# Conversions moved into attention, narrow gate products, and GpSimd's two-operand work given to VectorE

## The chip, the cores and the metric

The kernel runs on one core of a Trainium2 chip. The metric is the device time of one execution in microseconds (us). Engines are named as in the profile: PE is TensorE (matrix products, transposes), PEld its weight loads, DVE is VectorE, ACT is ScalarE, POOL is GpSimd, SP is SyncE, which here only issues transfers.

## The reference

Three layers follow each other.

```python
# 1. attention, 4 batches x 8 heads, 768 positions of 64 numbers:
#    a window of 15 neighbours on each side, and 24 block summaries (max of k, mean of v over 32 positions)
scores_all = concat([where(|i-j| < 16, q@k.T / 8, -1e9), q@k_sum.T / 8 + log(32)], -1)
x = softmax(scores_all) @ concat([v, v_sum])          # -> 3072 tokens x 512
# 2. mixture of 8 experts, each takes exactly 384 tokens, assigned greedily by descending gate value
logits = x @ w_gate                                    # 3072 x 8
out[mask_e] = relu(x[mask_e] @ w1[e]) @ w2[e]          # 512 -> 1024 -> 512
# 3. gated layer, all tokens
a, b = x @ moe2_w1, x @ moe2_w2                        # "gate weights" below: 512 x 1024 each, float64 inputs
y = ((a * b) @ moe2_w3) @ moe2_w_out                   # 1024 x 1024, 1024 x 512, float64 inputs
```

The matrices of layer 3 arrive in float64 and are turned into float32 on the core ("conversions"). The product of the two last ones, moe2_w3 @ moe2_w_out, is formed once on the core ("folds").

## The kernel before, in words

**The planner.** The kernel doesn't issue its instructions in the order of the program text. `body` describes every operation to `Plan`, with a due time (`at(t)`, in planned us) and a cost from `cost`. `Plan.run` then plays the engines forward on the host: whenever an engine is free it takes, among the operations whose inputs are ready, the one that is due first, and the order found is written out as fixed queues, one for each engine. Operations inside `urgent()` are "hot": an operation that isn't hot is held back if a hot one would become ready within `HOLD` ns while it ran. `SAFE`, `REL` and `LAG` are margins for semaphores and buffers: a buffer counts as free `REL` after its last reader, or `SAFE` for a VectorE operation that isn't hot and touches the routing's buffer `rt`.

**Attention.** 16 units (4 batches x 4 pairs of heads), each with three groups of four 64-row blocks. PE forms scores, transposes and outputs; ACT takes the exponential; POOL rearranges q and k. Behind each unit the gate product for its 128 columns is added into a PSUM tile `rt` (`GT`): six products of 128 tokens each, with the tokens' transposed values (`XT`, 128 x 128) as the stationary operand and the gate weights (128 x 8) as the moving one. Behind the fourth unit of a batch VectorE copies the tile to `LG`. Between these, spread over attention by due times, stand 32 conversions (`conv`) of 128 x 512 numbers: ACT and POOL take absolute values and limits, VectorE does two bit operations, POOL the last addition. Eight of them are for moe2_w_out, sixteen for moe2_w3 and 4 x `ND` = 8 for the gate weights, whose results are stored to device memory (`abd`).

**Behind attention.** `nc.swap` releases attention's buffers; operations described after it see `nc.bar` set. Then run, by due time: the routing of expert 0 (`routing(0)`, hot: six rounds of comparing on VectorE (`gq`), counting on PE, a new threshold (`need`, `ni`, `base`, `thr`, `pre`), then the list of tokens `idx`); seven folds (hot: transposes, 24 products of 512 columns, splits into a high and a low part on ACT and VectorE: `xh`, `xl`, `w`); the loads of the four stored gate weight rows (`load_ab`), each split by ACT (`ab`, high part) and POOL (low part); the remaining eight conversions (`conv_ab`), each followed by such a split. `AB0` and `ABD` set their due times. Expert 0's weights come by indirect transfers that POOL issues, as soon as the routing has named the expert.

**The experts.** Eight rounds of about 90 us: tokens gathered by `idx`, layer 1 and 2 of the expert (`l1`, `l2`), then the gate weights (`l3`) and the folded matrix (`l4`). Meanwhile the routing of the next expert runs, not hot. All recorded instructions have one line, L395, that of the planner's helper; they are told apart by their tiles.

Of the kernel before, what the change touches and what calls it, by code (L numbers as in the profile page):

```python
# [8 lines left out]
F32 = mybir.dt.float32  # L9
# [90 lines left out]
class Plan:  # L100
# [130 lines left out]
    def run(self):  # L231
# [22 lines left out]
        while todo:  # L254
            moved = False
            for e, (wait, q) in ready.items():
# [35 lines left out]
                    if e == "sync":  # L292
                        self.free[e] = max(t + dur, self.dma - DMA_AHEAD)
                slow = e == "vector" and i not in self.hots and any(b.name == "rt" for b in ops[i][3])
                heapq.heappush(ends, (done + (SAFE if slow else REL), i))
                order.append(i)
                self.done[i] = t
                todo -= 1
# [43 lines left out]
       "vector": {"tensor": 150, "scalar": 128, "gpsimd": 156, "sync": 120, "vector": 127},  # L342
       "gpsimd": {"tensor": 143, "scalar": 76, "vector": 80, "sync": 240}}

HOLD = 150.0

CALM, CALM_D = 500.0, 2000.0

# [2 lines left out]
SAFE = 600.0  # L351
# [95 lines left out]
def body(tc, q, k, v, w_gate, w1, w2, wa, wb, w3, wo, out):  # L447
# [22 lines left out]
    STEP, T0, TL, TE = 3.3, 243, 271, 87  # L470
    GATE, EARLY = 1, 0.0
    NF, TR, FT, FD = 1, 2, 245, 3
    NW, ND, AB0, ABD = 8, 2, 12, 3.9
    P_LD, P_MN, P_VL, P_PUT, P_VC, P_RL, P_TR, P_N = 24, 8, 14, 6, 11, 10, 10, 2
    P_ST, P_SC, P_C0, P_C1, P_CL, P_FO, P_FS = 8, 10, 10, 15, 6, 3, 5
    P_GA, P_SU, P_RW, P_W2, P_W20, P_RO, P_WC = 20, 16, 40, 16, 6, 15, 6
# [92 lines left out]
    with at(10):  # L569
        triu = cp.tile([128, 128], BF, name="triu")  # L570
        nc.vector.tensor_scalar(triu, jp, 0.0, None, op0=OP.is_gt)
        LG = cp.tile([128, C, E], F32, name="LG")
        WG = ap_.tile([128, DB, E], F32, name="wg")
        nc.sync.dma_start(WG, w_gate.rearrange("(c p) e -> p c e", p=128))


    def split_sb(hi, lo, raw, eng=None):
        nc.scalar.activation(hi, raw, AF.Copy)
        (eng or nc.gpsimd).tensor_tensor(lo, raw, hi.bitcast(F32), op=OP.subtract)

    def split_ps(hi, lo, ps):
        nc.scalar.activation(hi, ps, AF.Copy)
# [17 lines left out]
    def conv(src, r, h, dst, t, raw=None):  # L600

        with at(t - P_CL):
            if raw is None:
                stages.append(ap_.tile([128, 1024], F32, name="sta", bufs=2, fifo=True) if len(stages) % 2 else stage())
                raw = stages[-1]
            nc.sync.dma_start(raw.bitcast(I32), src[r * 128:(r + 1) * 128, h * 512:(h + 1) * 512].bitcast(I32))
        with at(t), nc.patient():
            w = raw.bitcast(I32).rearrange("p (a b) -> p a b", b=2)
            lo, hi = w[:, :, 0], w[:, :, 1]
            c = ap_.tile([128, 512], F32, name="ca", bufs=1) if nc.bar is None and len(stages) % 4 == 0 else ep.tile([128, 512], F32, name="a", bufs=3)  # L610
            nc.scalar.activation(c, hi.bitcast(F32), AF.Abs)
            nc.scalar.activation(lo, lo.bitcast(U32), AF.Copy, scale=2.0 ** -29)
            nc.gpsimd.tensor_scalar(c, c, 122879.9921875, 2.0 ** -15, op0=OP.min, op1=OP.max)
            a = c.bitcast(I32)
            nc.vector.tensor_scalar(a, a, 5, 2, op0=OP.logical_shift_left, op1=OP.logical_shift_right)
            nc.vector.scalar_tensor_tensor(a, hi, -1073741824, a, op0=OP.bitwise_and, op1=OP.bitwise_or)
            f = dst if dst is not None else c
            nc.gpsimd.tensor_tensor(f.bitcast(I32), a, lo, op=OP.add)
        return f

    WO, W3, WF = {}, {}, {}
# [119 lines left out]
    def group(G):  # L741
# [59 lines left out]
        if g == 2:  # L801
            with at(STEP * G + P_SC):
                if pr == 0:
                    GT[b] = pp.tile([128, 6, E], F32, name="rt", fifo=True)
                with nc.block():
                    for i in range(3):
                        for t in range(2):
                            nc.tensor.matmul(GT[b][:, 2 * i + t], XT[u, i][:, t], WG[:, pr], start=(pr == 0 and i + t == 0),
                                             stop=(pr == HP - 1 and i + t == 3))
        if pr == HP - 1 and g == 2:  # L810
            with at(STEP * G + P_SC):
                nc.vector.tensor_copy(LG[:, 6 * b:6 * b + 6, :], GT[b])

    for u in range(NU):
        prep(u)
# [505 lines left out]
```

## Time and profile before

| what | value |
|---|---|
| median of 3 runs | 1032.13 us (1030.18 to 1032.99) |
| the profiled execution, its own time | 1025.71 us |
| its span, first to last instruction | 1023.9 us |
| PE busy | 966.9 us (94%) |
| PEld busy | 877.7 us (86%) |
| DVE busy | 603.9 us (59%) |
| ACT busy | 409.8 us (40%) |
| POOL busy | 321.5 us (31%) |
| mean granted clock of TensorE | 0.982 of full speed |

Busy time is the union of an engine's instructions; PE's ends are modelled, so that two neighbouring products overlap in the list, and the time that one takes in a row of products is the distance of the starts. Attention runs from 0 to about 229 us, the stretch with the folds and the first routing from 229 to 298 us, the eight experts from there to the end.

### The profile page before, as it was taken

How to read it: one execution, taken by the hardware profiler on the slowest of the kernel's cores; microseconds unless marked ns; L12 is line 12 of the kernel's file. 1: busy time of each engine (PE TensorE's matmuls, PEld its weight loads, DVE VectorE, ACT ScalarE, POOL GpSimd, SP SyncE). 2: the span in 40 equal slices, each digit the busy share in tenths (PEclk: the TensorE clock that was granted, in tenths of full speed). 3: DMA queues.
4: the chain of work that ended last, by engine and by line, in shares of the span. 5: the costliest groups of instructions: out<-in, count | busy, mean ns of one | idle time of the engine just before them, and what ended most of it. 6: DMA issues, size and time to landing. Idle time of an engine off the chain costs nothing.

```text
span 1023.9 us, 17970 instructions
## 1 busy us (share of the span) xinstructions
PE 966.9 (94%) x6827; PEld 877.7 (86%) x6827; DVE 603.9 (59%) x1620; ACT 409.8 (40%) x961; POOL 321.5 (31%) x401
## 2 busy tenths in 40 slices
PE   6798989997989999999999999999999999999995
PEld 5688978775678899989989998998999899999994
DVE  5775576858877853882685388268538726323210
ACT  5786878864343233233223323222332323223211
POOL 9986466646623221041022104102210414001001
PEclk9998999998999999999999999999999999999998
DMA  8767778772141311040131105003110405101000
GB/s 235 193 181 204 207 210 257 208 232 112 32 164 42 125 52 52 1 165 31 33 121 54 52 2 165 32 32 111 65 52 1 165 21 165 42 11 52 1 1 31
DMA packets 81703, 100.06 MB, mean 98 GB/s; under 512 B 30416, under 2 KB 63696, under 8 KB 81616
## 3 DMA queue, kind: packets, MB, share of 16 engines
q1 hardware_dynamic: 68560, 52.76, 18.3%
q0 software_dynamic: 13056, 46.14, 13.6%
q8 instruction: 54, 0.88, 0.3%
q14 instruction: 33, 0.27, 0.1%
HBM read 81.81 MB, written 14.68 MB: 94 GB/s over the span
## 4 chain that ended last, share of the span: by engine, by line
PE 57%; issue 10%; DVE 7%; DMA 4%; ACT 2%; POOL 2%; POOLq 0%; ACTq 0%; SPq 0%; DVEq 0%
PE mm L395 32%; PE ac L395 23%; DMA ra<-in_moe_w_dram,iw 3%; PE rt L395 2%; POOL ra L1109 1%; DVE wl L395 1%; DVE gq L395 1%; DVE a L395 1%; DVE xl L395 1%; DMA abd<-ca 1%; ACT s L395 1%; DMA st<-in_moe_w_dram,iw 1%; DVE base L395 1%; ACT wh L395 1%; DVE pre L395 0%
## 5 line engine op out<-in xcount | busy, mean ns | idle before, releaser
L395 PE MATMUL mm<-xh,ab 128*128 128x384 f32 x1024 | 273.4, 338 | 0.0
L395 PEld LDWEIGHTS mm<-xh,ab 128*128 128x128 f32 x1024 | 185.5, 188 | 4.5 <-issue 3.3
L395 PE MATMUL mm<-xl,ab 128*128 128x384 f32 x512 | 174.4, 341 | 0.0
L395 PE MATMUL ac<-w,hh 128*128 128x512 f32 x384 | 123.6, 398 | 0.0
L395 DVE TENSOR_TENSOR a<-a,mm 128x384 f32<-128x384 f32 x64 | 35.2, 551 | 140.4 <-PE mm L395 117.9
L1109 POOL DMA_INDIRECT ra<-in_moe_w_dram,iw x32 | 31.4, 982 | 219.3 <-DVE go L395 190.9
L395 PEld LDWEIGHTS mm<-xl,ab 128*128 128x128 f32 x512 | 96.1, 188 | 3.0 <-DVE xl L395 1.1
L395 PE MATMUL mm<-xh,wh 128*128 128x384 f32 x256 | 88.1, 345 | 0.8 <-ACT xh L395 0.7
L395 PE MATMUL mm<-xl,wh 128*128 128x384 f32 x256 | 87.0, 340 | 0.0
L395 PE MATMUL ac<-hl,wh 128*128 128x384 f32 x256 | 87.0, 340 | 0.0
L395 PE MATMUL ac<-hh,wl 128*128 128x384 f32 x256 | 86.8, 339 | 0.0
L395 PE MATMUL mm<-xh,wl 128*128 128x384 f32 x256 | 86.6, 338 | 0.0
L395 ACT ACTIVATE a<-mm 128x384 f32<-128x384 f32 x64 | 31.3, 490 | 137.6 <-PE mm L395 137.6
L1109 POOL DMA_INDIRECT xg<-xd,idx x24 | 35.3, 1472 | 158.6 <-PE mm L395 119.4
L395 PE MATMUL ac<-hh,wh 128*128 128x384 f32 x256 | 84.5, 337 | 0.0
L1171 POOL DMA_INDIRECT out_dram<-a,idx x24 | 26.7, 1114 | 176.9 <-ACT a L395 173.7
L395 PEld LDWEIGHTS ac<-w,hh 128*128 128x128 f32 x384 | 70.9, 188 | 11.8
L395 ACT ACTIVATE hh<-a 128x384 fp32r<-128x384 f32 x64 | 33.5, 524 | 115.7 <-DVE a L395 115.7
L395 DVE TENSOR_TENSOR wl<-st,wh 128x512 fp32r<-128x512 f32 x64 | 44.0, 688 | 57.7 <-ACT wh L395 57.5
L395 PE MATMUL ac<-w,hl 128*128 128x512 f32 x192 | 76.4, 398 | 0.0
L395 DVE TENSOR_TENSOR wl<-ra,wh 128x512 fp32r<-128x512 f32 x64 | 43.9, 687 | 41.7 <-ACT wh L395 41.7
L395 ACT ACTIVATE wh<-ra 128x512 fp32r<-128x512 f32 x64 | 42.4, 664 | 62.2 <-PE mm L395 32.7
(271 smaller groups left out, 2078.8 us busy)
## 6 DMA issues: line engine op xcount, KB each, us to landing
st<-in_moe_w_dram SPq DMA_DIRECT2D x14, 512.0 KB
sta<-in_moe_w_dram SPq DMA_DIRECT2D x14, 512.0 KB
kn<-in_k_dram SPq DMA_DIRECT2D x32, 192.0 KB
qn<-in_q_dram SPq DMA_DIRECT2D x32, 192.0 KB
xd<-xo SPq DMA_DIRECT2D x16, 384.0 KB
vw<-in_v_dram SPq DMA_DIRECT2D x32, 176.0 KB
vw<-vs SPq DMA_DIRECT2D x64, 36.6 KB
st<-in_moe_w_out_dram SPq DMA_DIRECT2D x4, 512.0 KB
```

The costliest lines, as they stand in the source:

```text
L395: return getattr(real_engine, method)(*map(real, a), **{k: real(x) for k, x in kw.items()})
L1109: nc.add("gpsimd", lambda: tc.nc.gpsimd.indirect_dma_start(out=real(dst), out_offset=None, in_=real(src), in_offset=bass.IndirectOffsetOnA ...
L1171: s = tc.nc.gpsimd.indirect_dma_start(out=out, out_offset=bass.IndirectOffsetOnAxis(ap=real(idx), axis=0), in_=real(o), in_offset=None)
```

## The change

Four things change.

1. `ND` goes from 2 to 3: twelve of the sixteen gate weights' conversions stand in attention (36 conversions there in all), six instead of four rows are loaded by `load_ab`, and four instead of eight conversions are left behind. Their due times move back by 10 us (`AB0`). The staging tiles of those left all come from the pool `ep`.
2. The gate products are turned round: the gate weights, padded to 32 columns, are the stationary operand, and 256 tokens' values the moving one; three products for each unit write 32 partitions each of `GT`. Behind the fourth unit the result is copied to SBUF by ACT, transposed back by two transposes on PE and copied to `LG` by VectorE.
3. Behind attention (`nc.bar` set) the low parts of the splits and the last addition of a conversion run on VectorE instead of POOL.
4. The planner holds non-hot operations for a hot one that comes within 300 instead of 150 ns, and counts the routing buffer `rt` as free three times `SAFE` (1800 ns) behind a VectorE operation that isn't hot.

```diff
-                heapq.heappush(ends, (done + (SAFE if slow else REL), i))
+                heapq.heappush(ends, (done + (3 * SAFE if slow else REL), i))
...
-HOLD = 150.0
+HOLD = 300.0
...
-    NW, ND, AB0, ABD = 8, 2, 12, 3.9
+    NW, ND, AB0, ABD = 8, 3, 22, 3.9
...
-        WG = ap_.tile([128, DB, E], F32, name="wg")
-        nc.sync.dma_start(WG, w_gate.rearrange("(c p) e -> p c e", p=128))
+        WG = ap_.tile([128, DB, 32], F32, name="wg")
+        nc.gpsimd.memset(WG, 0.0)
+        nc.sync.dma_start(WG[:, :, 0:E], w_gate.rearrange("(c p) e -> p c e", p=128))
...
     def split_sb(hi, lo, raw, eng=None):
         nc.scalar.activation(hi, raw, AF.Copy)
-        (eng or nc.gpsimd).tensor_tensor(lo, raw, hi.bitcast(F32), op=OP.subtract)
+        (eng or (nc.gpsimd if nc.bar is None else nc.vector)).tensor_tensor(lo, raw, hi.bitcast(F32), op=OP.subtract)
...
-                stages.append(ap_.tile([128, 1024], F32, name="sta", bufs=2, fifo=True) if len(stages) % 2 else stage())
+                stages.append(ap_.tile([128, 1024], F32, name="sta", bufs=2, fifo=True) if nc.bar is None and len(stages) % 2 else stage())
...
             f = dst if dst is not None else c
-            nc.gpsimd.tensor_tensor(f.bitcast(I32), a, lo, op=OP.add)
+            (nc.gpsimd if nc.bar is None else nc.vector).tensor_tensor(f.bitcast(I32), a, lo, op=OP.add)
...
-                    GT[b] = pp.tile([128, 6, E], F32, name="rt", fifo=True)
+                    GT[b] = pp.tile([128, 256], F32, name="rt", fifo=True)
                 with nc.block():
                     for i in range(3):
-                        for t in range(2):
-                            nc.tensor.matmul(GT[b][:, 2 * i + t], XT[u, i][:, t], WG[:, pr], start=(pr == 0 and i + t == 0),
-                                             stop=(pr == HP - 1 and i + t == 3))
+                        nc.tensor.matmul(GT[b][32 * i:32 * i + 32], WG[:, pr], XT[u, i].rearrange("p t s -> p (t s)"),
+                                         start=(pr == 0), stop=(pr == HP - 1))
         if pr == HP - 1 and g == 2:
             with at(STEP * G + P_SC):
-                nc.vector.tensor_copy(LG[:, 6 * b:6 * b + 6, :], GT[b])
+                lt = ap_.tile([96, 256], F32, name="lt", bufs=1)
+                nc.scalar.activation(lt, GT[b][0:96], AF.Copy)
+                ps = pp.tile([128, 2, 96], F32, name="mm", bufs=3)
+                for t in range(2):
+                    nc.tensor.transpose(ps[:, t, :], lt[:, t * 128:(t + 1) * 128], ident[0:96, 0:96])
+                nc.vector.tensor_copy(LG[:, 6 * b:6 * b + 6, :].rearrange("p (g t) e -> p g t e", t=2),
+                                      ps.rearrange("p t (g r) -> p g t r", r=32)[:, :, :, 0:E])
```

## Rows read from the trace of the kernel before

**Rows 1.** Windows: stretch, its length; PE, PEld, DVE, ACT, POOL busy; PEclk, DMA share, GB/s.

```profile
50.00:215.00 165.00, 153.53 (x1829) 136.14 (x1829) 111.94 (x224) 132.04 (x402) 108.19 (x149) 0.95 0.77 211
...
229.00:298.00 69.00, 57.56 (x321) 41.38 (x322) 61.85 (x143) 30.92 (x55) 38.62 (x32) 0.95 0.31 111
...
298.00:331.00 33.00, 30.62 (x188) 29.34 (x188) 22.08 (x65) 11.43 (x21) 7.73 (x7) 0.95 0.17 53
...
388.00:478.00 90.00, 89.49 (x547) 82.88 (x546) 55.81 (x176) 26.23 (x50) 16.19 (x17) 1.00 0.19 65
```

**Rows 2.** Timeline of VectorE, 229 to 298 us: start, duration, operation, [idle before].

```profile
229.14 0.21 DVE L395 COPY LG<-rt 128x48 f32<-128x48 f32 x1 [3.95 <-PE rt L395]
...
243.15 3.36 DVE L395 TENSOR_TENSOR gq<-key,thr 128x768 bf16<-128x768 f32 x2
...
287.58 0.15 DVE L395 SCALAR_TENSOR_TENSOR idx<-i 128x3 int32<-128x3 f32 x1
```

**Rows 3.** Timeline of TensorE, 229 to 298 us, same columns.

```profile
245.29 0.33 PE L395 MATMUL rt<-oh,gq 128*128 128x16 bf16 x6 [5.04 <-DVE gq L395]
...
297.77 1.41 PE L395 MATMUL mm<-xh,wh 128*128 128x384 f32 x3 [0.69 <-ACT xh L395]
```

**Rows 4.** Groups of VectorE, 229 to 298 us.

```profile
L395 DVE TENSOR_TENSOR gq<-key,thr 128x768 bf16<-128x768 f32 x9 | 10.0, 1120 | 0.0
...
L395 DVE TENSOR_TENSOR pre<-js,base 128x32 int32<-128x32 int32 x4 | 3.9, 977 | 0.1
...
L395 DVE SCALAR_TENSOR_TENSOR a<-ab,a 128x512 int32<-128x512 int32 x4 | 3.7, 930 | 0.1
L395 DVE SCALAR_TENSOR_TENSOR base<-ni,base 128x1 int32<-128x1 int32 x4 | 3.7, 915 | 0.1
L395 DVE TENSOR_TENSOR wl<-ra,wh 128x512 fp32r<-128x512 f32 x5 | 3.3, 681 | 0.0
L395 DVE TENSOR_SCALAR a<-a 128x512 int32<-128x512 int32 x4 | 2.4, 604 | 0.0
```

**Rows 5.** Groups of VectorE, 478 to 568 us, where GpSimd has no two-operand work.

```profile
L395 DVE TENSOR_TENSOR gq<-key,thr 128x768 bf16<-128x768 f32 x8 | 7.5, 952 | 0.0
...
L395 DVE TENSOR_TENSOR pre<-js,base 128x32 int32<-128x32 int32 x4 | 0.8, 190 | 0.1
...
L395 DVE SCALAR_TENSOR_TENSOR base<-ni,base 128x1 int32<-128x1 int32 x4 | 0.6, 160 | 0.1
```

**Rows 6.** Groups of GpSimd, 230 to 298 us.

```profile
L395 POOL TENSOR_TENSOR ab<-ab,ab 128x512 fp32r<-128x512 f32 x8 | 11.2, 1410 | 7.0 <-ACT ab L395 7.0
L395 POOL TENSOR_TENSOR ab<-a,ab 128x512 fp32r<-128x512 f32 x6 | 8.3, 1405 | 3.3 <-ACT ab L395 3.3
```

**Rows 7.** Timeline of TensorE inside attention, 154 to 162 us.

```profile
154.97 0.49 PE L395 MATMUL mm<-ident,kr 128*128 128x128 f32 x3
155.39 0.88 PE L395 MATMUL mm<-vw,ind 96*32 96x130 f32 x24
156.19 0.69 PE L395 MATMUL ac<-vw,pt 121*64 121x65 f32 x16
...
159.32 1.50 PE L395 MATMUL rt<-wg,xt 128*128 128x8 f32 x12
160.68 0.42 PE L395 MATMUL mm<-ident,xo 128*128 128x128 f32 x2
160.93 0.49 PE L395 MATMUL mm<-ident,qr 128*128 128x128 f32 x3
161.26 0.37 PE L395 MATMUL ac<-mv,sel 67*128 67x480 bf16 x1
```

**Rows 8.** Groups of GpSimd, 0 to 229 us: count, busy us, mean ns, idle before.

```profile
L395 POOL TENSOR_SCALAR a<-a 128x512 f32<-128x512 f32 x26 | 16.5, 635 | 9.8 <-ACT a L395 8.0 <-DVE rs L395 0.9
...
L395 POOL TENSOR_TENSOR a<-a,st 128x512 int32<-128x512 int32 x8 | 10.8, 1346 | 2.4 <-ACT pt L395 1.8 <-ACT sta L395 0.7
```

**Rows 9.** Who waited for whom on TensorE, 345 us to the end: total, times, longest.

```profile
PE rt L395 <- DVE i L395: 3.0, 5, 0.8
```

## The prediction

> **What bounds the kernel now.** I first cut the span into stages with the windows view [rows 1]. From 388 to 478 us, one expert of seven alike, TensorE is busy for 89.5 of 90 us at its full clock: nothing but its own work can be gained there. In attention (50 to 215 us) it is busy for 153.5 of 165 us, with ScalarE at 132, VectorE at 112 and GpSimd at 108: several engines are near their limit and TensorE is nearest. From 229 to 298 us it idles for 11.4 of 69 us, and its granted clock averages 0.95, so about 6.9 us ran at 1.2 instead of 2.4 GHz. VectorE is busy for 61.9 of those 69 us, 90%. That stretch is where the kernel loses time.
>
> Then the timelines. The stretch begins with the last copy of gate values at 229.14; the routing delivers the token list at 287.58, 58.4 us later [rows 2], and expert 0's first product starts at 297.77 [rows 3]. TensorE's queue is fixed and holds routing products between fold products, so when the routing is late the folds stand behind it: at 245.29 it had waited 5.04 us for the comparisons `gq`, two of which took 3.36 us together [rows 2, 3].
>
> The same instructions by group show why. In the stretch `pre` takes 977 ns, `base` (one number per partition) 915 and `gq` 1120 [rows 4]; in an expert's round, where GpSimd does nothing with two operands, they take 190, 160 and 952 [rows 5]. In the stretch GpSimd runs 14 low parts of splits of 1.4 us each [rows 6]. An instruction of VectorE with two operands in SBUF seems to stand until GpSimd's has ended.
>
> **The change part by part.**
>
> *Gate products.* A block of six now takes 160.68 - 159.32 = 1.36 us [rows 7]. The nearest row for the new form is the block for the means: also 32 columns wide and f32, twelve products of 130 columns over four column groups, in 156.19 - 155.39 = 0.80 us [rows 7]. That is three rounds of 0.267 us, four products side by side. One round of 256 columns is 0.267 x 256/130 = 0.53 us, and the three new products write three different groups, so I take 0.53; if they ran one behind the other it would be 1.58. Sixteen blocks save 13.4 us of TensorE, or cost 3.5. Eight new transposes at 0.11 us (three in 0.33, 161.26 - 160.93 [rows 7]) cost 0.9. TensorE frees 12.5 us.
>
> How much of that shortens attention? All, if TensorE alone set the pace; but it idles for 11.5 of 165 us already, waiting for others, and ScalarE stands at 80% [rows 1]. I take a third, 4 us. On the path to the routing the last product is 0.83 us shorter, while a copy by ScalarE and two transposes (0.22) come ahead of the 0.21 us copy [rows 2]; I put this at nothing, give or take 0.8.
>
> The three transposes in front of the narrow block take 155.39 - 154.97 = 0.42 us, the three in front of a full-width product 0.33 [rows 7]: entering the narrow form costs some 0.09 us. The Trainium skill, page TensorEngine Tiling (Array Packing), section Key Properties, says that a change of tiling mode drains TensorE. By that rule each new block pays twice; at 0.09 us that is 32 x 0.09 = 2.9 us of the 12.5, a third of it in the sum, which would then be 1 us later. I leave it out, since a fixed queue may set the block next to another narrow one.
>
> *Four more conversions in attention.* Each costs GpSimd 0.635 + 1.346 = 1.98 us [rows 8], the most of any engine, together 7.9. GpSimd is busy for 66% of 50 to 215 us and the transfers for 77% [rows 1], so most of it hides there; if that cover were gone, all 7.9 us would show. I take a fifth, 1.5 us. Each also brings a load and a store on SP's queue, ahead of which nothing waits but later loads. Attention in sum: 4 - 1.5 = 2.5 us earlier; bounds 12.5 earlier and 7.9 later (11.4 if the narrow products don't overlap).
>
> *GpSimd's two-operand work on VectorE.* It gives back the time in which VectorE stood: four `pre` at 0.79, four `base` at 0.755, nine `gq` at 0.17: 7.7 us [rows 4, 5], nearly all of it in the chain of the routing. Behind it goes TensorE's wait of 5.04 us [rows 3] and the low clock after it. What TensorE could gain at most from 229 to 331 us is its idle time, 11.4 + 2.4, and half of the time at the lower clock, 3.4 + 1.7: 18.9 us [rows 1].
>
> VectorE pays for it. A low part with 512 columns takes it 0.68 us, as `wl` does [rows 4]; sixteen are 10.9 us, four last additions 2.7. Two of the conversions that are left disappear, (0.604 + 0.930) x 2 = 3.1 us [rows 4]. From 229 to 331 us it has 61.9 + 22.1 = 84.0 us of work [rows 1]; afterwards 84.0 - 7.7 + 10.9 + 2.7 - 3.1 = 86.8. At the 90% that it reached in the stretch, this fits into 96.8 instead of 102 us: only 5.2 us come out. But the new work is due 10 us later and is not hot, so it can fill the 10.9 us that VectorE idles from 298 to 331 us [rows 1], and expert 1's routing, needed only for the round after, can slip. Between 5.2 and 18.9 I take 9, nearer the bound by VectorE. What is late next is the first product of `l3`, which needs all sixteen splits. Fewer loads or more of them change little: the transfers are busy for 31% there [rows 1].
>
> *The planner.* The longer margin for `rt` moves routing products in the experts' rounds back in TensorE's queue. Five waits of TensorE for `i` are 3.0 us [rows 9], and they are the only ones recorded there. I take 2 of the 3, bounds 0 and 3. The longer hold acts on hot neighbours only, in the stretch, and is inside the 9.
>
> *Sum.* 2.5 + 9 + 2 = 13.5 us. The profiled execution took 1025.71 us, its span plus 1.8 for what lies around it; that is 6.4 us below the median of 1032.13. From its own time the sum gives 1012.2; set against the median, in whose terms I forecast, 1018.6 us.
>
> **The rivals.**
>
> *Attention gives nothing.* The narrow products don't overlap (3.5 us lost) and the conversions cost their 1.5: 5 us later instead of 2.5 earlier, so 1032.1 + 5 - 9 - 2 = 1026 us. For it: their LDWEIGHTS are of the same weights and each has 128 rows, unlike the means'. Against: the 0.80 us of the means. 0.15.
>
> *Everything comes through.* TensorE sets attention's pace, 8 us there, 13 in the stretch, 3 with the experts: 1008 us. For it: 93% busy in attention. Against: ScalarE at 80% and VectorE's load of 86.8 us. 0.12.
>
> *The stretch doesn't shrink.* VectorE, now with 86.8 us of work, is filled up to `l3`, and what it no longer loses by standing it spends on splits: 1032.1 - 2.5 - 2 = 1027.6 us. For it: its 90%. Against: what can slip. 0.12.
>
> *Slower: the splits stand in front of the routing.* If the fixed order of VectorE has the sixteen low parts and four additions between the copy at 229 and the token list, as GpSimd ran most of them [rows 6], the chain of the routing gets 20 x 0.68 = 13.6 us of foreign work for the 7.7 that it is freed of: 5.9 longer, and TensorE, waiting, runs some 5 us more at the lower clock (2.5 lost). With 4.5 gained elsewhere that is 1032.1 + 8.4 - 4.5 = 1036 us. It decides from about 19 of the 20 in the chain; with 11 of them the chain only breaks even. Against: due 10 us later, not hot, held back up to 300 ns. 0.09.
>
> **How the numbers follow.** My forecast has 0.52, with its own range of 1013 to 1024 us. A measurement of this kernel can tell some 0.3%, 3.1 us, from no change. Faster than 1029: the forecast 0.52, the full gain 0.12, 0.12 of the first rival and 0.04 of the third, 0.80. Within: 0.03 of the first and 0.07 of the third, 0.10. Slower: 0.10, the last rival and a rest. The range from 1008 to 1031 leaves out half of the full gain and the slower case, and holds the unknown costs between: attention from 10 earlier to 5 later with the stretch at 9.
>
> **What the profile would show.** Right: no two-operand group of GpSimd behind some 230 us, except none or one straggler; `pre` and `base` near 0.2 us in the stretch; no wait of 5 us on TensorE and a granted clock nearer 1 there; the token list some 45 to 50 us behind the gate copy; blocks of three gate products spaced about 0.5 us; the waits for `i` gone. Wrong: narrow blocks above 1.3 us; the last gate copy later than 229 us, with conversions still running behind it; splits between `need` and `base` in VectorE's timeline; a wait of TensorE before `l3`'s first product; experts' rounds longer than 90 us. The attention term is the one that I trust least, because a list of due times can shift all queues.

## The result, and the profile after

The changed kernel takes 1005.9 us (median of 4 runs, 1005.6 to 1007.0) beside 1031.2 for the kernel before on the same chip (4 runs, 1028.8 to 1033.0): a ratio of 0.976, with a 95% interval of 0.974 to 0.978. It is 25 us faster where 13.5 were forecast, and 2 us below the range. Its profiled execution took 1005.94 us, with a span of 1004.2; that of before took 1025.71, which is 5.5 us below the median that it is compared with. So the two profiles, whose spans differ by 19.7 us, show all of the gain but these 5.5 us.

Where the 19.7 us come from is read off three events: the last copy to `LG`, the start of expert 1 and that of expert 6; the token list `idx` stands between the first two. First the windows of the changed kernel, the columns as in [rows 1]; the last but one of these lines spans expert 0's first part, the last one a later round.

```profile
50.00:215.00 165.00, 146.71 (x1850) 123.06 (x1848) 120.93 (x237) 140.17 (x419) 110.72 (x149) 0.99 0.80 225
75.00:150.00 75.00, 68.37 (x895) 58.40 (x894) 55.27 (x111) 65.71 (x203) 50.08 (x70) 1.00 0.81 223
215.00:230.00 15.00, 7.52 (x36) 5.34 (x36) 13.82 (x22) 4.75 (x9) 7.17 (x6) 0.61 0.63 192
220.00:283.00 63.00, 56.07 (x312) 40.66 (x310) 58.14 (x151) 28.14 (x51) 18.86 (x15) 0.93 0.42 145
283.00:331.00 48.00, 45.24 (x293) 43.05 (x293) 38.55 (x122) 15.92 (x30) 2.40 (x3) 1.00 0.14 45
375.00:465.00 90.00, 89.97 (x550) 83.52 (x549) 55.88 (x175) 27.00 (x52) 15.33 (x18) 1.00 0.19 65
```

Two of these stretches of the kernel before, same view:

```profile
75.00:150.00 75.00, 69.61 (x818) 62.27 (x817) 46.37 (x98) 57.17 (x176) 45.39 (x63) 0.91 0.77 202
215.00:230.00 15.00, 13.32 (x121) 11.20 (x120) 7.67 (x20) 7.72 (x20) 5.12 (x5) 1.00 0.75 228
```

Against [rows 1], TensorE is busy for 6.8 us less between 50 and 215 us while ScalarE and VectorE work 8 and 9 us more in the same time: attention runs faster. In its middle the granted clock is 1.00 instead of 0.91. At its end, between 215 and 230 us, there is a new hole: TensorE is busy for half of the time and the granted clock averages 0.61, so that it stands at the lower of its two levels (1.2 instead of 2.4 GHz) for most of it. Over the whole stretch, 220 to 283 us, the clock is 0.93.

VectorE's timeline of the changed kernel, 219 to 284 us (start, duration, operation), beside [rows 2]:

```profile
220.10 0.20 DVE L395 COPY LG<-mm 128x48 f32<-128x48 f32 x1
...
220.72 1.10 DVE L395 TENSOR_TENSOR eq<-LG,key 128x192 f32<-128x192 f32 x1
...
224.04 2.92 DVE L395 TENSOR_TENSOR gq<-key,thr 128x768 bf16<-128x768 f32 x2
...
238.22 0.49 DVE L395 SCALAR_TENSOR_TENSOR base<-ni,base 128x1 int32<-128x1 int32 x1
238.84 0.19 DVE L395 TENSOR_TENSOR pre<-js,base 128x32 int32<-128x32 int32 x1
...
247.64 0.35 DVE L395 TENSOR_TENSOR need<-need,rt 32x8 f32<-32x8 f32 x2
248.02 0.15 DVE L395 TENSOR_TENSOR sat<-rt,need 31x8 bf16<-31x8 f32 x1
248.10 0.67 DVE L395 TENSOR_TENSOR ab<-a,ab 128x512 fp32r<-128x512 f32 x1
248.70 0.67 DVE L395 TENSOR_TENSOR ab<-ab,ab 128x512 fp32r<-128x512 f32 x1
249.31 0.15 DVE L395 TENSOR_REDUCE ni<-rt 128x1 int32<-128x8 f32 x1
249.49 0.16 DVE L395 SCALAR_TENSOR_TENSOR base<-ni,base 128x1 int32<-128x1 int32 x1
...
272.53 0.15 DVE L395 SCALAR_TENSOR_TENSOR idx<-i 128x3 int32<-128x3 f32 x1
```

The copy stands at 220.10 instead of 229.14: attention gives 9.0 us. From copy to list it is 52.4 instead of 58.4 us. The lines at 248 us show that low parts of splits (`ab`) stand inside the routing, between `need` and `base`. TensorE's timeline of the changed kernel, in attention and then at its end, answers to [rows 7] and [rows 3]:

```profile
117.19 0.63 PE L395 MATMUL rt<-xt,wg 128*32 128x256 f32 x6
117.75 0.44 PE L395 MATMUL mm<-ident,xo 128*128 128x128 f32 x2
...
217.97 0.58 PE L395 MATMUL mm<-ident,lt 96*128 96x96 f32 x2 [2.61 <-ACT lt L395]
225.05 0.31 PE L395 MATMUL rt<-oh,gq 128*128 128x16 bf16 x6 [3.57 <-DVE gq L395]
...
248.66 0.17 PE L395 MATMUL rt<-sat,onesb 31*128 31x8 bf16 x1
...
283.77 1.17 PE L395 MATMUL mm<-xh,wh 128*128 128x384 f32 x3 [0.69 <-ACT xh L395]
```

A gate block takes 117.75 - 117.19 = 0.56 us. The wait of 5.04 us for `gq` [rows 3] has become one of 3.57 us, and a wait of 2.61 us for ScalarE's copy `lt` is new. Expert 0 starts at 283.77, 14.0 us earlier than before.

GpSimd's timeline at the same place shows what is left of attention there, two last additions of conversions, which read two operands:

```profile
220.32 1.29 POOL L395 TENSOR_TENSOR a<-a,st 128x512 int32<-128x512 int32 x1 [1.15 <-issue]
222.23 0.61 POOL L395 TENSOR_SCALAR ca<-ca 128x512 f32<-128x512 f32 x1 [0.63 <-DVE eq L395]
224.26 1.88 POOL L395 TENSOR_TENSOR ca<-ca,sta 128x512 int32<-128x512 int32 x1 [1.41 <-ACT xh L395]
```

The two `gq` that start at 224.04 take 2.92 us, where two undisturbed ones take 1.9 [rows 5]: the second addition runs beside them. `eq` at 220.72, with 192 columns, takes 1.10 us beside the first one. The groups of VectorE from 220 to 283 us, columns as in [rows 4]:

```profile
L395 DVE TENSOR_TENSOR gq<-key,thr 128x768 bf16<-128x768 f32 x8 | 9.0, 1140 | 0.0
L395 DVE TENSOR_TENSOR ab<-ab,ab 128x512 fp32r<-128x512 f32 x12 | 8.0, 680 | 0.0
...
L395 DVE SCALAR_TENSOR_TENSOR base<-ni,base 128x1 int32<-128x1 int32 x4 | 0.9, 237 | 0.1
L395 DVE TENSOR_TENSOR pre<-js,base 128x32 int32<-128x32 int32 x4 | 0.7, 185 | 0.1
```

`base` fell from 915 to 237 ns and `pre` from 977 to 185. Last the rounds, by the chain of waits: TensorE's chains of 24 products by which experts 1, 2, 3 and 6 begin, of the changed kernel,

```profile
375.62 4.18 PE mm L395 x24
...
464.98 4.18 PE mm L395 x24
...
554.34 4.18 PE mm L395 x24
...
822.44 4.18 PE mm L395 x24
```

and of the kernel before:

```profile
391.88 4.18 PE mm L395 x24
...
481.82 4.18 PE mm L395 x24
...
571.96 4.18 PE mm L395 x24
...
842.16 4.18 PE mm L395 x24
```

From expert 1 to expert 6 a round takes 89.36 instead of 90.06 us on average. Expert 1 begins at 375.62 instead of 391.88, 16.3 us earlier: 9.0 from attention and 7.2 from the stretch with expert 0. Five more rounds add 3.5 us, and from there to the end both take 182 us. 9.0 + 7.2 + 3.5 = 19.7.

### The profile page after: what moved, and what is told of

It is laid out like the page before. It is cut to its first block, busy times and chain, and to the rows that moved or that the text cites. A ratio compares the mean times of both kernels' runs of the same rounds, so it can differ in the third digit from the quotient of the medians.

```text
span 1004.2 us, 17849 instructions
## 1 busy us (share of the span) xinstructions
PE 945.2 (94%) x6739; PEld 854.2 (85%) x6739; DVE 610.8 (61%) x1640; ACT 412.0 (41%) x965; POOL 290.4 (29%) x382
## 3 DMA queue, kind: packets, MB, share of 16 engines
q0 software_dynamic: 13056, 46.14, 13.9%
## 4 chain that ended last, share of the span: by engine, by line
PE 67%; issue 10%; DVE 8%; DMA 5%; ACT 4%; POOL 3%; SPq 1%; POOLq 0%; DVEq 0%; ACTq 0%
PE mm L395 37%; PE ac L395 28%; PE rt L395 2%; DVE a L395 2%; DMA st<-in_moe_w_dram 2%; DMA sta<-in_moe_w_dram 1%; DVE gq L395 1%; ACT s L395 1%; DMA xg<-xd,idx 1%; POOL a L395 1%; DMA vw<-vs 1%; ACT kw L395 1%; DMA st<-in_moe_w_dram,iw 1%; DVE kw L395 1%; DVE mx L395 1%
## 5 line engine op out<-in xcount | busy, mean ns | idle before, releaser
L395 PE MATMUL mm<-xh,ab 128*128 128x384 f32 x1024 | 276.8, 339 | 0.0
L395 PE MATMUL ac<-w,hh 128*128 128x512 f32 x384 | 120.2, 394 | 0.0
L1115 POOL DMA_INDIRECT xg<-xd,idx x24 | 25.3, 1056 | 149.0 <-PE mm L395 110.9
L395 ACT ACTIVATE hh<-mm 128x384 fp32r<-128x384 f32 x64 | 30.7, 480 | 80.5 <-PE mm L395 80.5
```

Source lines behind the costliest of these rows:

```text
L395: return getattr(real_engine, method)(*map(real, a), **{k: real(x) for k, x in kw.items()})
L1115: nc.add("gpsimd", lambda: tc.nc.gpsimd.indirect_dma_start(out=real(dst), out_offset=None, in_=real(src), in_offset=bass.IndirectOffsetOnA ...
```

## The experiments

Times are medians beside the kernel before on the same chip, which took 1027 to 1033 us there. "Copy" and "list" are the times of the copy to `LG` and of `idx` in the one profile of each run. The ratios are those on record; that of the two medians can differ from them by up to 0.004.

**The four parts alone.** Each was put into the kernel before by itself, the gate products and the conversions with the staging tiles of the change.

```diff
-                            nc.tensor.matmul(GT[b][:, 2 * i + t], XT[u, i][:, t], WG[:, pr], start=(pr == 0 and i + t == 0),
-                                             stop=(pr == HP - 1 and i + t == 3))
+                        nc.tensor.matmul(GT[b][32 * i:32 * i + 32], WG[:, pr], XT[u, i].rearrange("p t s -> p (t s)"),
+                                         start=(pr == 0), stop=(pr == HP - 1))
...
-    NW, ND, AB0, ABD = 8, 2, 12, 3.9
+    NW, ND, AB0, ABD = 8, 3, 22, 3.9
...
-        (eng or nc.gpsimd).tensor_tensor(lo, raw, hi.bitcast(F32), op=OP.subtract)
+        (eng or (nc.gpsimd if nc.bar is None else nc.vector)).tensor_tensor(lo, raw, hi.bitcast(F32), op=OP.subtract)
...
-                heapq.heappush(ends, (done + (SAFE if slow else REL), i))
+                heapq.heappush(ends, (done + (3 * SAFE if slow else REL), i))
```

The first run has the first of these edits, with the padded `WG`, the new `GT` and the way back through `lt`; the second run the second; the third run the third, and the last addition of a conversion on VectorE; the fourth run the last, and `HOLD = 300.0`.

> Only the gate products are turned round (and behind attention all staging tiles come from the pool ep, as in the changed kernel). Theory: TensorE sets the pace of attention, so most of the 12.5 us that it is freed of come out: the last gate copy at 217 to 220 us instead of 229, the run 8 to 12 us faster. Rival, the step of the prediction: a third comes out, copy at 225, run 4 us faster, and the rest of the 9 us of the whole change came from another edit. If neither, the copy stays at 229 and the order of the queues did it.

> Only ND 3, AB0 22 and the staging tiles from ep; the gate products stay wide and GpSimd keeps its two-operand work. Theory: four more conversions hide in attention, which ends within 2 us of before, and the shorter work behind it gives 0 to 4 us, so the run is 0 to 4 us faster. Rival: GpSimd, 1.98 us for each conversion, lengthens attention by up to 8 us and the run is 3 to 8 us slower.

> Only the low parts of the splits and the last additions behind attention go to VectorE; all else as before. Theory: `base` and `pre` fall from 0.9 to about 0.2 us, the token list comes 6 to 10 us sooner behind the gate copy, the run is 5 to 9 us faster. Rival (VectorE's load is the bound): the blocked time is spent on the 13.6 us of new work, the run within 2 us of before. Second question: the kernel before took 1025.7 us when profiled and 1028.8 to 1033.0 otherwise, the changed one 1005.6 to 1007.1. If the spread comes from VectorE standing behind GpSimd, this kernel's runs agree within 1.5 us and its median gains some 5 us more than its profile.

> Only the two margins of the planner (three times SAFE for rt, HOLD 300). Theory: the wait of TensorE for `i` in each expert's round goes, rounds shorten from 89.9 to 89.4 us, the run is 3 to 4 us faster, attention and the stretch as before within 1 us. Rival: the wait only moves to another routing product, the run within 1 us of before.

| part | time, us | ratio to before (95%) | copy | copy to list |
|---|---|---|---|---|
| gate products | 1015.6 | 0.989 (0.983 to 0.995) | 221.5 | 55.6 |
| conversions | 1019.4 | 0.993 (0.990 to 0.995) | 226.3 | 53.2 |
| work to VectorE | 1023.8 | 0.997 (0.994 to 1.000) | 227.4 | 50.6 |
| planner | 1022.9 | 0.998 (0.995 to 1.002) | 226.8 | 56.6 |

By the ratios the parts gain 11.0, 7.6, 3.2 and 1.6 us, together 23 (by the medians 12.4, 8.5, 4.2 and 5.1, together 30); the gate products are the largest, and the conversions, which I had priced as a cost in attention, gain by themselves: their way from copy to list is 5.2 us shorter than before's 58.4, with fewer of GpSimd's two-operand instructions left beside the routing (their later due times are in this run too). With the planner's part alone a round takes 89.38 us in the profile, as with the whole change; five such rounds save 3.4 us, although the ratio can't tell the part from nothing. The work on VectorE shortens the way from copy to list by 7.8 us in the profile, but only 3.2 of it (0 to 6.4) arrive at the end by the ratio.

**The change without one part.** The changed kernel again, and three times with one part undone.

```diff
-                    GT[b] = pp.tile([128, 256], F32, name="rt", fifo=True)
+                    GT[b] = pp.tile([128, 6, E], F32, name="rt", fifo=True)
...
-    NW, ND, AB0, ABD = 8, 3, 22, 3.9
+    NW, ND, AB0, ABD = 8, 2, 22, 3.9
...
-            (nc.gpsimd if nc.bar is None else nc.vector).tensor_tensor(f.bitcast(I32), a, lo, op=OP.add)
+            nc.gpsimd.tensor_tensor(f.bitcast(I32), a, lo, op=OP.add)
```

The first edit stands for all hunks of the gate products, the third for both of GpSimd's, the splits too.

> The changed kernel once more, as the measure for the next three on the same chip. Expected: 24 to 27 us faster than before, runs within 2 us of each other. Theory on the spread: attention's runs differ by how long TensorE is at the lower clock there; where the granted clock of 75 to 150 us is 1.00 the last gate copy comes at 219 to 221 us in every execution.

> The change without the turned gate products. Theory: TensorE sets attention's pace; the copy comes 5 to 8 us later than in the changed kernel and the run takes 6 to 12 us more. Rival (the conversions' place set attention's end, ScalarE and GpSimd its pace): the run takes under 3 us more.

> The change with ND 2 again (AB0 stays 22): eight conversions in attention, eight behind it on VectorE. Theory: VectorE behind attention is the bound there, and four more conversions with both additions cost it about 4 x 1.8 = 7 us, so the run takes 4 to 8 us more. Rival (attention pays for the conversions what the stretch saves): within 2 us of the changed kernel.

> The change with the low parts and the last additions back on GpSimd. Theory: `base` and `pre` rise to 0.9 us again, the token list comes 4 to 8 us later behind the copy, the run takes 4 to 8 us more. Rival (VectorE's own load is the bound, the blocked time is only swapped for work): within 2 us of the changed kernel.

| kernel | time, us | ratio to before (95%) | copy | copy to list |
|---|---|---|---|---|
| changed | 1006.5 | 0.980 (0.974 to 0.987) | 222.0 | 52.9 |
| wide gate products | 1013.6 | 0.989 (0.985 to 0.992) | 224.7 | 49.1 |
| eight conversions in attention | 1002.9 | 0.977 (0.971 to 0.984) | 219.3 | 49.2 |
| two-operand work on GpSimd | 1017.1 | 0.990 (0.987 to 0.992) | 219.8 | 64.9 |

By the medians the wide gate products cost 7.1 us, and all ten of their times (1010.3 to 1018.9) lie above the changed kernel's (1005.1 to 1008.2). The profile caught the fastest of the ten and the slowest of the changed kernel's four; these two are 2.0 us apart, and the list even comes 1 us earlier with the wide products, so most of the 7.1 us can't be read off them. Handing the work back to GpSimd costs 10.6 us, and all of it lies between copy and list. The groups of that kernel behind attention, VectorE and then GpSimd, show the old picture:

```profile
L395 DVE TENSOR_TENSOR gq<-key,thr 128x768 bf16<-128x768 f32 x10 | 13.8, 1394 | 0.0
...
L395 DVE TENSOR_TENSOR pre<-js,base 128x32 int32<-128x32 int32 x4 | 3.2, 810 | 0.1
L395 DVE SCALAR_TENSOR_TENSOR base<-ni,base 128x1 int32<-128x1 int32 x4 | 2.3, 585 | 0.1
```

```profile
L395 POOL TENSOR_TENSOR ab<-ab,ab 128x512 fp32r<-128x512 f32 x12 | 16.9, 1419 | 11.3 <-ACT ab L395 11.3
```

The four further conversions gain 7.6 us alone and cost 3.6 us inside the change (the intervals of the two ratios overlap; the times themselves, 1001.3 to 1003.8 beside 1005.1 to 1008.2, don't). The windows from 215 to 230 us, columns as in [rows 1], show a difference at the end of attention: first the changed kernel measured beside them, then the one with eight conversions.

```profile
215.00:230.00 15.00, 7.30 (x31) 4.14 (x32) 14.18 (x18) 5.34 (x11) 9.21 (x8) 0.50 0.52 176
```

```profile
215.00:230.00 15.00, 10.75 (x63) 7.41 (x62) 11.85 (x28) 7.39 (x14) 3.79 (x5) 0.89 0.70 240
```

With twelve, GpSimd is busy for 9.2 of these 15 us with what is left of attention's conversions, TensorE is busy for only 7.3 and runs at 1.2 GHz throughout, a granted clock of 0.50. With eight it is 3.8 and 10.8 us. Once GpSimd has no more two-operand work behind attention, moving conversions forward takes nothing off the routing, and only their cost remains. That cost belongs to how this attention ends rather than to the number alone: the kernel with wide products has twelve conversions too, its list comes 49.1 us behind the copy, and its clock between 215 and 230 us is 1.00.

In attention itself the four further conversions cost nothing that the copies show. By their timelines the kernels below fall into four groups, and within a group the queues of attention hold the same order; each number is the copy in one profile.

| gate products | eight conversions | twelve conversions |
|---|---|---|
| wide | 229.1, 227.4, 226.8 (before, work to VectorE, planner) | 226.3, 224.7 (conversions, wide gate products) |
| narrow | 221.5, 219.3 (gate products, eight conversions) | 220.1, 222.0, 219.8 (changed, changed again, two-operand work on GpSimd) |

Equal queues differ by some 2 us. Beside that, twelve conversions come no later than eight in either row, and the narrow products bring 7.4 us on average with eight and 4.9 with twelve.

**TensorE's work against the order of the queues.** The gate products gained so much more than a third of their work that I first took TensorE to set attention's pace. Two extra rounds of narrow products with zero weights were to test that.

```diff
+                    for n in range(2):
+                        for i in range(3):
+                            nc.tensor.matmul(GT[b][32 * i:32 * i + 32], WZ, XT[u, i].rearrange("p t s -> p (t s)"),
+                                             start=False, stop=(pr == HP - 1 and n == 1))
```

> The changed kernel with two more rounds of narrow products in every block, on a stationary tile of zeros, so that they add nothing: 0.56 us of TensorE for each round, 16 x 1.12 = 17.9 us more in all. Theory: TensorE sets attention's pace for most of its length; half or more of it shows, the last gate copy at 229 us or later instead of 220 to 222, the run 8 to 15 us slower than the changed kernel. Rival, the prediction's third: copy 6 us later or less.

It took 1018.9 us (ratio 0.992, 0.989 to 0.995), with the copy at 237.35: 15 to 17 us later than in the two profiles of the changed kernel. That looked like the whole of the added work. But the extra products also have a cost in the planner, and the queues of this kernel are ordered otherwise. The next three keep the two apart: with a factor on the planned cost of a block (1/2 with one extra round, as shown, 1/3 with two, 3 without any), the first two have exactly the queue order of the changed kernel and more work, the third its work and another order.

```diff
-    def block(self):
+    def block(self, k=1.0):
...
-                 [v for p in parts for v in p[2]], sum(p[3] for p in parts), 0.0)
+                 [v for p in parts for v in p[2]], k * sum(p[3] for p in parts), 0.0)
...
-                with nc.block():
+                with nc.block(1 / 2):
```

> The changed kernel with one extra round of three narrow products with zero weights in each of the sixteen gate blocks (it adds zeros), while the planner still counts a block at its old cost, so every queue keeps the order of the changed kernel. TensorE gets 16 x 0.56 = 9.0 us more work in attention. If TensorE sets attention's pace in this order, the last gate copy comes 7 to 9 us behind that of the changed kernel (220.1 and 222.0 us in two profiles), at 228 to 231, and the time is 1013 to 1015 us. If the 15 to 17 us that three times the gate products showed came mostly from another order of the queues, and only a third of TensorE's work shows, the copy comes at 223 to 225 and the time is about 1009 us.

> The same with two extra rounds: 17.9 us more of TensorE's work in attention, in the order of the changed kernel. If TensorE sets the pace, the copy comes 14 to 18 us later, at 235 to 239, and the time is 1020 to 1024 us; TensorE's idle time between 50 and 215 us stays near the 18 us of the changed kernel or falls. If a third shows, the copy comes at 227 and the time is about 1012 us, and TensorE's idle time falls by some 10 us.

> The changed kernel's own products, but the planner counts each gate block at three times its cost: the order of the queues is that of a kernel with longer gate products, the work is that of the changed kernel. If the order is worth little beside TensorE's work, the copy comes within 3 us of the changed kernel's 220 to 222 and the time is 1003 to 1009 us. If the order was most of what three times the gate products cost, the copy comes at 230 or later and the time is 1014 us or more.

| kernel | time, us | ratio to before (95%) | copy |
|---|---|---|---|
| one extra round, same order | 1010.5 | 0.981 (0.978 to 0.984) | 224.66 |
| two extra rounds, same order | 1014.8 | 0.986 (0.983 to 0.988) | 229.05 |
| order alone | 1019.4 | 0.990 (0.987 to 0.993) | 233.23 |

The work added was less than I had put down. TensorE's timeline of the kernel with two extra rounds:

```profile
122.39 1.50 PE L395 MATMUL rt<-xt,wg 128*32 128x256 f32 x18
123.82 0.44 PE L395 MATMUL mm<-ident,xo 128*128 128x128 f32 x2
```

A block takes 123.82 - 122.39 = 1.43 us, 0.87 more than 0.56, so a round is 0.435 us and the two kernels add 7.0 and 13.9 us, not 9.0 and 17.9. Beside the changed kernel's 1006.2 (the mean of its two medians) they take 4.3 and 8.6 us longer, six tenths of the added work; by the ratios to the kernel before it is 3.2 and 7.7 us, about a half. Their copies come 3.6 and 8.0 us later than the mean of the changed kernel's two. The run with three times the gate products adds the same 13.9 us, yet its copy came 15 to 17 us later, so the work alone can't be the reason. And the order alone, with no work added, delays the copy by 11 to 13 us. That kernel and the one with three times the products were planned with nearly the same costs, but by their timelines the orders part at some 64 us, so that the 4.1 us between their copies are not the work alone. Both theories fell: TensorE doesn't set the pace by itself, and in the changed kernel's order a third was too little.

Two runs tried the same around the kernel before: fewer gate products in its exact order, and the narrow products ordered with the planned cost of the wide ones.

```diff
-    def block(self):
+    def block(self, n=None):
...
-        fns = [p[0] for p in parts]
+        fns = [p[0] for p in parts][:n]
...
-                with nc.block():
+                with nc.block(None if pr in (0, 3) else 1):
```

> The kernel before, in its own order, with 40 of its 96 gate products left out: behind the second and third unit of a batch only the first of six is done, so the gate values lack parts of their sums, while every queue and every wait stays. TensorE has 40 x 0.227 = 9.1 us less work in attention. If two fifths of TensorE's work show, as the extra rounds in the changed kernel's order say (2.7 to 4.6 of 9.0, 7 to 9 of 17.9 us), the gate copy comes 3 to 5 us before the 229.1 of before (or before the 226.8 to 227.4 of the two kernels that share its order in attention), at 223 to 226, and the time is 1024 to 1028 us beside 1029. If TensorE sets the pace, the copy comes at 218 to 220 and the time is 1018 to 1022 us.

> The kernel before with the gate products turned round and the staging tiles of the change, as in the run with the gate alone, but the planner counts a block at the cost of the old form, 1298 instead of 457 ns, and without a change of form. The work is that of the run with the gate alone, the order another one. If the gain there (copy at 221.5 us, 1015.6 us) came from TensorE's work, this run repeats it within 2 us. If two fifths of the work show and the rest was the order that true costs give, the copy comes at 224 us or later and the time is 1019 to 1027 us.

With fewer products it took 1029.0 us beside 1032.7 (ratio 0.996, 0.993 to 0.999): 4.4 us gained, 1.2 to 7.6, of some 8.5 us of work. That is half, with a wide interval, and agrees with a half to six tenths better than with a pace set by TensorE, which would have given 8 or 9. Its profiled execution took 1033.55 us and had the copy at 234.4; it was the longest of ten and its copy tells nothing. With the narrow products in another order the time was 1025.5 us (0.995, 0.992 to 0.998), a gain of 5.5 us (2.6 to 8.5) where the planner's own costs had given 11.0 (5.0 to 17). The work is the same in both, and the copy comes at 225.9 instead of 221.5, so several microseconds of the gate products' gain are likely order; the two intervals overlap, so neither this nor how many is settled.

**Due times.** If order is worth that much, the conversions' due times, which spread them over attention, are a cheap handle. `P_C1` sets how early the last of them is due, `ND` how many there are. The first run has the first edit, the second both; the third has `ND = 1` alone.

```diff
-    P_ST, P_SC, P_C0, P_C1, P_CL, P_FO, P_FS = 8, 10, 10, 15, 6, 3, 5
+    P_ST, P_SC, P_C0, P_C1, P_CL, P_FO, P_FS = 8, 10, 10, 35, 6, 3, 5
...
-    NW, ND, AB0, ABD = 8, 3, 22, 3.9
+    NW, ND, AB0, ABD = 8, 2, 22, 3.9
```

> The changed kernel with the 36 conversions due in 180 instead of 200 planned us (P_C1 35 for 15). Theory: in the changed kernel the last of them run at 222 to 228 us, when attention has ended, and stand between the gate copy and the first comparisons; with them earlier TensorE's wait of 3.6 to 3.8 us for the first comparison goes and the run is 2 to 5 us faster than the changed kernel. Rival: they press on attention instead, whose copy comes later by what the seam gains.

> Eight conversions of gate weights in attention (ND 2) and these due earlier (P_C1 35), the rest as in the changed kernel. Theory: the wait of 2.9 us for the first comparison that ND 2 alone still has goes too; 1 to 4 us faster than with ND 2 alone (1002.9 us). Rival: nothing is left to gain there, within 1 us of it.

> Four conversions of gate weights in attention (ND 1), twelve behind it on VectorE, the rest as in the changed kernel. Theory: each four conversions that leave attention shorten its end by 2 to 3 us, but cost VectorE 7 us behind it, where it is 95% busy with ND 2; the run 2 to 6 us slower than with ND 2. Rival (the fewer in attention the better): 3 us faster than with ND 2.

| kernel | time, us | ratio to before (95%) | copy | copy to list |
|---|---|---|---|---|
| twelve, due earlier | 1011.0 | 0.982 (0.976 to 0.988) | 227.8 | 52.7 |
| eight, due earlier | 998.9 | 0.972 (0.967 to 0.977) | 215.2 | 50.2 |
| four | 1015.5 | 0.989 (0.983 to 0.995) | 224.6 | 49.8 |

The same shift of due times brings the copy 6 to 8 us later with twelve conversions and 4 us earlier with eight. With twelve the profile is the slowest of four executions from 1005.7 to 1013.8 us, so the shift there may be smaller: by the medians the kernel is 4.8 us slower. Four in attention are 12 us slower than eight, by the ratios 0.989 and 0.977, and more than the 2 to 6 us that I had expected: their copy is 5.3 us later though fewer stand there, which points to the order once more. Eight, due earlier, is the fastest kernel of this study, at 998.9 us (997.9 to 1000.4, 4 runs), 7 us below the changed kernel.

## Why the prediction was wrong

The direction was right, and so were the mechanisms of the stretch and of the rounds; the time fell below the range because attention gave far more than its term, and because of what the sum was set against. Against the two profiles: attention 9.0 us where 2.5 were forecast, the stretch 7.2 where 9, the experts 3.5 where 2.

**Attention, the step that failed: "I take a third, 4 us".** The price of a block was nearly right: 0.53 forecast, 0.56 measured, a round of 0.435 and 0.13 that a block takes besides its rounds, where I had read 0.09 for entering the narrow form off [rows 7]. The Trainium skill says that a change of tiling mode drains TensorE (page TensorEngine Tiling (Array Packing), section Key Properties). The runs agree that a block costs something besides its rounds, 0.13 us; sixteen are 2 us, inside the 0.56. That it is the drain is not shown. The wide block was one of the longer ones: of before's sixteen the middle one takes 1.27 and not 1.36 us. So TensorE frees (1.27 - 0.56) x 16 - 0.9 = 10.5 us, not 12.5. Of that, a half to six tenths show by the runs in fixed order: 5.3 to 6.3 us in place of 4. My reason for a third, that TensorE already idles for 11.5 of 165 us, was no measure: an engine that waits now and then can still stand in most of the chains.

**The order had no term.** I wrote that a list of due times can shift all queues and gave it no price. Another order of the same work cost 11 to 13 us, and a shift of due times moved the copy by 4 to 8 us either way. The two profiles of the changed kernel show 7.1 and 9.0 us in attention. The work saved explains 5.3 to 6.3 of them, and the conversions take nothing off that the copies show. The rest, some 1 to 4 us, is what neither explains. The order that the new costs gave and the clock, 0.91 before and 1.00 after in the middle of attention, are both there; how it divides between them stays open.

**Conversions.** The 1.5 us for attention were too much: the copies with eight and with twelve overlap (219.3 and 221.5 beside 219.8 to 222.0). But with eight the time is 3.6 us lower, and the list comes 49.2 instead of 52.4 and 52.9 us behind the copy. What I had not seen is that their remains end up beside the first comparisons, where I had forecast "no two-operand group of GpSimd behind some 230 us, except none or one straggler". There are two stragglers, and TensorE's wait of 3.57 us and its low clock stand beside them.

**GpSimd's two-operand work.** This step held. `pre` and `base` came to 185 and 237 ns (0.2 forecast), and the list 52.4 us behind the copy, where I had looked for 45 to 50; the changed kernel without this part loses 10.6 us, between copy and list. The Trainium skill has the rule (page SBUF — State Buffer, section Who interferes with whom): a VectorE instruction with two inputs in SBUF contends with a GpSimd instruction that reads SBUF. The run with the work back on GpSimd agrees: `base`, one number per partition, takes 585 ns there beside instructions of 1419 ns, and 237 without them. The stretch gave 7.2 and not 9 us; the hole at attention's end, with its waits of 2.61 and 3.57 us and its low clock, likely took part of it back, for where attention ends with a smaller hole or none the list comes 49.2 and 49.1 us behind the copy. So the sign "a granted clock nearer 1 there" failed, 0.93 after 0.95; the rival in which the stretch wouldn't shrink, VectorE being full, is refuted, although VectorE is busy for 58.1 of 63 us.

**The planner.** 2 us were forecast, 3.5 came in the profiles (a round 0.7 us shorter, and no wait for `i` left on TensorE). By the ratio the part alone could not be told from nothing, 1.6 us with an interval from 5.3 faster to 2.1 slower; by the medians it is 5.1 us faster.

**The sum was set against the wrong time.** I took 13.5 us from the median of before, 6.4 us above the profile that I had read. The step was consistent only if the changed kernel varied as before does. It doesn't: four executions lie within 1.5 us, its profile at their median. From the profile's own time the forecast would have been 1012.2, and the terms would have had to hold 19.7 us instead of 25.3.

The rivals: "everything comes through" (8, 13 and 3 us, 1008 us) was nearest, though by another split; "attention gives nothing" fell with the blocks of 0.56 us, and the last one, splits in front of the routing, was right about the order and wrong about its price. Eleven low parts and two last additions of the twenty do stand between copy and list, and some between `need` and `base`, which I had named a sign of being wrong. But the list still comes 6.0 us sooner behind the copy, and where they can be followed they run while VectorE would have to wait for TensorE's count: the two low parts at 248.10 and 248.70 end at 249.37, and the count that `ni` needs starts at 248.66.

## What to carry to other kernels

Where a planner writes the queues from costs, a cheaper instruction changes the order of everything: price the order as a term of its own, with a range of several microseconds, and tell it from the work by holding the planned cost fixed while the work changes. An engine that is busy for 93% and still waits gave back a half to six tenths of what it was spared here; measure that share with a few added instructions before choosing a fraction. Moving two-operand work off GpSimd pays where a chain of short VectorE instructions runs beside it, and once it is done, other ways of emptying GpSimd there stop paying. Two profiles with equal queues put the same copy 2 us apart, so a term of that size needs more than one pair of them. And a sum of differences read off one profile belongs to that execution's time: set against a median that lies elsewhere, it carries the gap along.

## What the hardware showed that I had not expected

Executions of one program differ with the granted clock. In the ten runs of the kernel with fewer gate products the fastest took 1021.69 us at a mean granted clock of 0.986, the slowest 1033.55 at 0.977: 0.009 of 1022 us is 9.2 us of work at full speed, beside 11.9 us of difference. The kernel before, measured beside it, spread over 12 us (1024.7 to 1036.9), the changed kernel over 1.5 and 3.1 us in its two series. Its clock between 75 and 150 us was 1.00 in both profiles, that of before 0.91. Narrow gate products alone don't make it so, since the kernel that has them in another order spread over 8 us, and neither does VectorE's freedom from GpSimd, since the kernel with that alone spread over 9. By the profiles the clock goes with the order of the queues: it is 1.00 in the middle of attention in all seven profiles that have the order of the changed kernel or that of the wide products with twelve conversions, 0.89 to 0.95 in the four with the order of before, and 0.93 to 0.98 in three other orders with narrow products and twelve conversions. What in an order decides it was not found.
